# A recurrence and its experts: transposes under sums, four sums moved, narrower turns

## The chip, the cores and the metric

The kernel runs on one core of a Trainium2 chip. The metric is the device time of one execution in microseconds (us), here the median of three runs. Engines are named as in the profile: PE (matmuls), PEld (its weight loads), DVE (vector), ACT (scalar), POOL (GpSimd), SP (issues DMAs).

## The reference

A gated linear recurrence with complex decay feeds a mixture of experts that takes the best one of eight for each token.

```
# B=4 batches, H=8 heads, S=768 steps, D=48
for t in range(S):
    new_re = ar*S_re - ai*S_im ; new_im = ar*S_im + ai*S_re
    S_re, S_im = new_re + k[t] (x) v[t], new_im
    y[t] = q[t] @ S_re
x = y as rows: 3072 tokens of 384
logits = x @ w_gate ; expert = argmax ; gate = softmax of it
for every expert e: rows of its tokens, in order, at most `capacity`
    y_e = relu(rows @ w1[e]) @ w2[e]      # 384 -> 1024 -> 384
out[token] = gate * y_e[its row]
```

## The kernel before

**Units.** The sequence is cut into 8 chunks of 96 steps, so there are 32 units, one for each batch and chunk; batches 0 and 1 come first, alternating, then 2 and 3. A unit loads its decayed q and k (`qkc`, from the scratch `scr`), transposes them per head (`tr`, L348), makes a masked 96x96 product (`pa`, L356), carries the state from chunk to chunk (L369 and after), and sums the output into `py` (L412, L417), with the 384 features in 4 blocks of two heads, each head on 64 partitions of which 48 are used. `take` copies that to `xt` (L590), `logits` multiplies by the gate weights (L612), copies the result to `lt` (L613), and `turn` (L600 to 604) transposes the four blocks back to 96 rows of tokens, which ACT copies to `x`, leaving out the unused columns.

**Order.** The list `SLOT_B` writes out, for one step, which stage of which unit comes next. From the second half of the recurrence to the last unit, PE, DVE, ACT and SP issue in the order of the program (`manual_schedule`); for the experts after that only SP does, and a planner orders the other engines.

**Routing.** After certain chunks `Route.route` runs four stages: R0 `logits` (PE `lg` L681, copy on ACT), R1 `choose` (DVE, L686 to L697), R2 `count` (PE `pp`, L702 and L704) and R3 `place` (DVE, L710 to L713, giving the row `slot` of each token). Rows of tokens are then scattered into `disp` by an indirect DMA of POOL (L622).

**The join.** Expert 0's rows are loaded from `disp` to `xr` (L807) before the last four chunks are there (`LATE`: chunks 7 and 8 of batches 2 and 3). `shift(k)` turns `xr` into PSUM by matmuls against the identity (L831; four blocks of 112 rows for each of the three k). For the late chunks DVE makes a 96x448 matrix of zeros and ones from `slot` (`own`, L821), and `spread` splits the rows into a high and a low part (L639 on ACT, L640 on DVE). `early(k)` adds the first two late chunks onto the same PSUM (two parts each, so four matmuls, L825), `end(k)` the last two, and copies the sum to `xh` and `xl` (L841, L842). In the program all three `shift` follow stage R0 of the last routing; R1, the last splits, R2 and R3 follow; then all `early`, all `end`, then the gates, the counts, and `sort`, whose result says which expert's weights are loaded next.

**Experts.** For each expert, PE turns its rows (`mt`, L911, here by `transpose`), makes `ph` (L973) and `my` (L981), and turns the result back (`yt`, L935).

Of the kernel before, what the change touches and what calls it, by code (L numbers as in the profile page):

```python
# [17 lines left out]
B, H, S, D = 4, 8, 768, 48  # L18
C = 96
DP = 64  # L20
NC = S // C
SIZES = (8, 16, 16, 16, 16, 16, 8)
SL = max(SIZES)
# [4 lines left out]
DM = H * D  # L28
# [24 lines left out]
def crossed(a):  # L53

    p, d = a.ap
    return bass.AP(a.tensor, a.offset, [list(p), [-D, 2], [D, 2], list(d)])


class Att:
# [262 lines left out]
    def unit(self, b, c):  # L322
# [81 lines left out]
        def y():  # L404
# [4 lines left out]
            for i in range(0, H, 2):  # L409
                for h in (i, i + 1):  # L410
                    o = h % 2 * DP
                    nc.tensor.matmul(out=py[o:o + DP, i // 2 * C:i // 2 * C + C], lhsT=v[:, h * D:h * D + DP],  # L412
                                     rhs=a_sb[:, h, :], start=True, stop=c == 0)
# [93 lines left out]
TP = 112  # L507
NT = T // TP
KT = DM // 128
# [8 lines left out]
class Route:  # L518
# [74 lines left out]
    def turn(self, b, c, xt):  # L593

        nc = self.nc
        if b == 3:
            self.x[b] = self.x[0]
        elif b not in self.x:
            self.x[b] = self.x_pool.tile([C, NC, XW], F32, tag="x", name=f"x_{b}", bufs=2)
        pt = self.ps.tile([C, 512], F32, tag="tr", name=f"x_{b}_{c}", bufs=2)  # L600
        for k in range(H // 2):
            nc.tensor.transpose(out=pt[:, k * 128:k * 128 + 128], in_=xt[:, k], identity=self.ident)  # L602
        nc.scalar.copy(out=self.x[b][:, c, :DM].rearrange("t (h e) -> t h e", h=H),
                       in_=pt.rearrange("t (h e) -> t h e", h=H)[:, :, :D])

    def logits(self, b, c, xt, pl):
        nc = self.nc
# [169 lines left out]
class Moe:  # L777
# [31 lines left out]
    def turn_ops(self, ps, chunks, parts, room):  # L809

        nc = self.nc
        acc, own = [], {}
        st = self.first = {t: self.p_0.tile([128, KT, T], F32R, name=f"{t}_0") for t in ("xh", "xl")}

        def find(b, c, slot):
            if len(own) < len(chunks) - 1:
                t = self.p_0.tile([C, T], F32R, name=f"own{len(own)}")
            else:
                t = room.rearrange("p h x -> p (h x)")[:C, :T].bitcast(F32R)
            own[b, c] = t  # L820
            nc.vector.tensor_scalar(out=t, in0=self.number, scalar1=slot, scalar2=None, op0=ALU.is_equal)  # L821

        def add(k, i, stop):
            for z, x in enumerate(parts[chunks[i]]):
                nc.tensor.matmul(out=acc[k][:, :T], lhsT=x[:, k * 128:k * 128 + 128], rhs=own[chunks[i]], start=False, stop=stop and z == 1)  # L825

        def shift(k):
            tag, bufs = (("pa", 2), ("pa", 2), ("s", 1))[k]
            acc.append(ps.tile([128, 512], F32, tag=tag, name=f"mt_0_{k}", bufs=bufs))
            for t in range(NT):  # L830
                nc.tensor.matmul(out=acc[k][:, t * TP:t * TP + TP], lhsT=self.xr[:, t, k * 128:k * 128 + 128],  # L831
                                 rhs=self.ident[:TP, :TP], start=t == 0, stop=False)

        def early(k):
            for i in range(len(chunks) - 2):
                add(k, i, False)

        def end(k):
            for i in range(len(chunks) - 2, len(chunks)):
                add(k, i, i == len(chunks) - 1)  # L840
            nc.scalar.copy(out=st['xh'][:, k], in_=acc[k][:, :T])  # L841
            nc.vector.tensor_tensor(out=st['xl'][:, k], in0=acc[k][:, :T], in1=st['xh'][:, k].bitcast(F32), op=ALU.subtract)  # L842

        def gates():
            st['tail'] = self.p_0.tile([TP, NT, XW - DM], F32, name="tail_0")
            nc.sync.dma_start(out=st['tail'], in_=self.disp[:T, DM:].rearrange("(t p) x -> p t x", p=TP))
        return find, shift, early, end, gates

    def open(self, ctx):
# [407 lines left out]
def kernel(ctx, tc, q, k, v, a_re, a_im, w_gate, w1, w2, out):  # L1257
    nc = tc.nc
    const = ctx.enter_context(tc.tile_pool(name="const", bufs=1))
    dram = ctx.enter_context(tc.tile_pool(name="dram", bufs=1, space=DRAM))  # L1260
    ident = const.tile([128, 128], F32, name="ident")
    flag = const.tile([1, 1], I32, name="flag")
    box = {}
    with ExitStack() as c_main, ExitStack() as c_att:
        cp = c_main.enter_context(tc.tile_pool(name="cp", bufs=1))
        x_pool = c_main.enter_context(tc.tile_pool(name="x_pool", bufs=1))
        att = Att(cp, c_att, tc, dram, ident, q, k, v, a_re, a_im)
        disp = dram.tile([E_ * T, XW], F32, name="disp")
        route = att.route = Route(tc, cp, x_pool, att.ps, ident, disp, w_gate, T, CUTS, LATE)
        with ExitStack() as c_moe:  # L1270
            with ExitStack() as c_dve:
                att.open_dve(c_dve)
                hand = {mybir.EngineType.PE, mybir.EngineType.DVE, mybir.EngineType.Activation, mybir.EngineType.SP}
                slots = att.slots()
                ops = att.dve_ops(slots, 6.5, 10.25)
                with tc.manual_schedule(engines={mybir.EngineType.DVE, mybir.EngineType.Activation}):
                    for op in ops[:att.begin]:
                        op()
                with tc.manual_schedule(engines={mybir.EngineType.DVE}):
                    for op in ops[att.begin:81]:  # L1280
                        op()
                    route.constants()
                    clear = route.clear_ops() + att.clear_ops()
                    for i, op in enumerate(ops[81:att.half], 81):
                        op()
                        if i % 8 == 0 and clear:
                            clear.pop(0)()
                    assert not clear
                with tc.manual_schedule(engines=hand):
                    for op in ops[att.half:]:  # L1290
                        op()
            att.third(c_att)
            moe = Moe(c_moe, tc, ident, disp, w1, w2, out)
            with tc.manual_schedule(engines=hand):
                room = [att.bufs["qkc"][i] for i in range(3)]
                route.room = room[:2]
                route.hook, shift, early, end, gates = moe.turn_ops(att.ps, LATE, route.parts, room[2])
                todo = [(14.5, lambda: nc.vector.memset(room[2][C:], 0.0)), (20, moe.numbers)]
                for p in range(Moe.NP):
                    at = 16 + 3 * p  # L1300
                    todo += [(at, lambda p=p: part(p))]
                todo.sort(key=lambda x: x[0])

                def part(p):
                    loads, splits = moe.weight_ops(0, p)
                    loads[0]()
                    n = 16 + 3 * p
                    todo.extend([(n + 1.5, loads[1]), (n + 2.5, splits[0]), (n + 3, splits[1]), (n + 4, splits[2]), (n + 4.5, splits[3])])
                    todo.sort(key=lambda x: x[0])
                loaded = False  # L1310
                for i, (n, op, _) in enumerate(slots):
                    while todo and todo[0][0] <= n:
                        todo.pop(0)[1]()
                    op()
                    if n > 30.8 and not loaded:
                        moe.load()
                        loaded = True
                    if i == len(slots) - 9:
                        for kk in range(KT):
                            shift(kk)  # L1320
                assert not todo and not route.ready
                for kk in range(KT):
                    early(kk)
                for kk in range(KT):
                    end(kk)
                route.rest()
                while route.ready:
                    route.pace()
                route.totals()
                gates()  # L1330
            route.sort()
            moe.order = route.order
            covered = uncovered(nc, cp, att.sums, att.small, route, flag)
            c_att.close()
            moe.open(c_moe)
            moe.run(lambda: covered(moe.ps))
    go = nc.values_load(flag, min_val=0, max_val=1)
    with tc.If(go > 0):
        General(tc, dram, ident, q, k, v, a_re, a_im, w_gate, w1, w2, out)
# [27 lines left out]
```

## Time and profile before

| | |
|---|---|
| median of three runs | 675.2 us (674.87 to 676.08) |
| the profiled execution's own time | 677.57 us |
| its span, first to last instruction | 675.9 us |
| PE busy | 547.2 us (81%) |
| DVE busy | 481.0 us (71%) |
| ACT busy | 345.8 us (51%) |
| POOL busy | 93.0 us (14%) |
| mean granted clock of PE | 0.923 |

The span is what the trace shows; the 1.67 us between it and the execution's own time lie outside the instructions. A granted clock of 1.00 is 2.4 GHz. Busy shares are means over stages with different limits: the recurrence fills DVE, the later units and the experts fill PE. In the chain views a row's time is what it adds to the chain, from the end of the row before to its own end; in the source and timeline views it is the instruction's own duration, and matmuls overlap.

### The profile page before, as it was taken

How to read it: one execution, taken by the hardware profiler on the slowest of the kernel's cores; microseconds unless marked ns; L12 is line 12 of the kernel's file. 1: busy time of each engine (PE TensorE's matmuls, PEld its weight loads, DVE VectorE, ACT ScalarE, POOL GpSimd, SP SyncE). 2: the span in 40 equal slices, each digit the busy share in tenths (PEclk: the TensorE clock that was granted, in tenths of full speed). 3: DMA queues.
4: the chain of work that ended last, by engine and by line, in shares of the span. 5: the costliest groups of instructions: out<-in, count | busy, mean ns of one | idle time of the engine just before them, and what ended most of it. 6: DMA issues, size and time to landing. Idle time of an engine off the chain costs nothing.

```text
span 675.9 us, 12575 instructions
## 1 busy us (share of the span) xinstructions
PE 547.2 (81%) x4455; PEld 472.2 (70%) x4455; DVE 481.0 (71%) x1432; ACT 345.8 (51%) x789; POOL 93.0 (14%) x140
## 2 busy tenths in 40 slices
PE   0344423366799998989999999999999999999994
PEld 0122211134577877779999988888999999999993
DVE  5999999999999998946757686365555655465431
ACT  6455443475788897644555553254344443443420
POOL 8030000000000000001222222101111202021111
PEclk9876566775999999999999999999999999999998
DMA  5199443585676788687888742483535353626101
GB/s 187 52 312 331 170 140 127 189 236 157 159 240 188 172 225 227 194 206 165 205 231 218 196 122 78 108 258 92 191 107 166 112 165 104 197 74 213 37 35 35
DMA packets 73239, 111.89 MB, mean 166 GB/s; under 512 B 6402, under 2 KB 63045, under 8 KB 71888
## 3 DMA queue, kind: packets, MB, share of 16 engines
q1 hardware_dynamic: 66384, 77.13, 42.0%
q0 software_dynamic: 6784, 33.88, 14.9%
q8 instruction: 37, 0.61, 0.4%
q14 instruction: 34, 0.28, 0.1%
HBM read 72.99 MB, written 34.26 MB: 159 GB/s over the span
## 4 chain that ended last, share of the span: by engine, by line
PE 62%; DVE 17%; ACT 10%; DMA 5%; issue 4%; POOL 1%; SPq 0%; POOLq 0%; DVEq 0%; ACTq 0%
PE ph L973 15%; PE my L981 14%; PE xp L132 5%; PE tr L348 4%; PE pa L356 4%; DVE xy L215 3%; PE s L369 3%; DMA qkc<-scr 3%; PE y L412 3%; DVE a L226 2%; PE y L417 2%; PE x L602 2%; DVE qko L286 2%; PE my L995 2%; PE wp L132 2%
## 5 line engine op out<-in xcount | busy, mean ns | idle before, releaser
L132 PE MATMUL xp<-a,ident 128*128 128x384 f32 x84 | 52.1, 791 | 93.3 <-ACT a L159 93.2
L872 DVE TENSOR_TENSOR lo<-raw,hi 128x384 fp32r<-128x384 f32 (+2 forms) x128 | 66.5, 554 | 64.9 <-ACT hi L871 55.2
L132 PEld LDWEIGHTS xp<-a,ident 128*128 128x128 f32 x84 | 24.4, 307 | 114.6 <-ACT a L159 81.5
L871 ACT CAST hi<-raw 128x384 fp32r<-128x384 f32 (+2 forms) x128 | 60.0, 512 | 55.4 <-PE ph L973 42.5
L215 DVE TENSOR_TENSOR xy<-a 128x96 f32<-128x96 f32 (+1 forms) x301 | 74.9, 279 | 0.7
L348 PE MATMUL tr<-ident,qkc 96*96 96x96 f32 x512 | 65.4, 251 | 9.6 <-DMA qkc<-scr 4.6
L973 PE MATMUL ph<-xh,hi 128*128 128x448 f32 (+4 forms) x192 | 69.7, 365 | 1.1 <-DVE hl L1019 1.1
L973 PE MATMUL ph<-xl,hi 128*128 128x448 f32 (+4 forms) x192 | 67.8, 353 | 0.0
L973 PE MATMUL ph<-xh,lo 128*128 128x448 f32 (+4 forms) x192 | 67.7, 353 | 0.0
L1019 DVE SCALAR_TENSOR_TENSOR hl<-ph,hh 128x448 fp32r<-128x448 f32 (+4 forms) x64 | 37.5, 587 | 39.1 <-ACT hh L1018 38.0
L1018 ACT ACTIVATE hh<-ph 128x448 fp32r<-128x448 f32 (+4 forms) x64 | 32.9, 515 | 61.0 <-PE ph L973 60.6
L981 PE MATMUL my<-hl,hi 128*128 128x448 f32 (+4 forms) x168 | 60.2, 358 | 0.0
L981 PE MATMUL my<-hh,lo 128*128 128x448 f32 (+4 forms) x168 | 59.9, 356 | 0.0
L348 PEld LDWEIGHTS tr<-ident,qkc 96*96 96x96 f32 x512 | 47.5, 128 | 16.6 <-ACT kT L350 7.7
L981 PE MATMUL my<-hh,hi 128*128 128x448 f32 (+4 forms) x168 | 56.2, 361 | 0.1
L226 DVE TENSOR_TENSOR a<-xy 128x48 f32<-128x48 f32 (+1 forms) x298 | 55.3, 215 | 0.4
L356 PE MATMUL pa<-qT,kT 128*96 128x96 f32 x512 | 54.3, 249 | 0.4 <-DVE a_sb L360 0.4
L356 PEld LDWEIGHTS pa<-qT,kT 128*96 128x96 f32 x512 | 49.8, 166 | 1.7 <-issue 1.4
L946 POOL DMA_INDIRECT out_dram<-o,xr x26 | 28.9, 1113 | 157.6 <-DVE o L945 155.8
L622 POOL DMA_INDIRECT disp<-x,idx x32 | 30.2, 943 | 111.6 <-DVE idx L621 59.8
L412 PE MATMUL y<-a_sb,v 128*64 128x96 f32 x512 | 42.3, 253 | 3.9 <-ACT lt L613 2.8
L369 PE MATMUL s<-v,qkc 128*96 128x96 f32 x448 | 44.2, 253 | 0.0
(196 smaller groups left out, 1185.4 us busy)
## 6 DMA issues: line engine op xcount, KB each, us to landing
raw<-in_moe_w_dram SPq DMA_DIRECT2D x64, 384.0 KB
qkc<-scr SPq DMA_DIRECT2D x32, 528.0 KB
scr<-qko POOLq DMA_DIRECT2D x10, 1536.0 KB, 6.8
disp<-fill POOLq DMA_DIRECT2D x7, 772.0 KB, 15.2
v<-in_v_dram SPq DMA_DIRECT2D x32, 144.0 KB
xr<-disp SPq DMA_DIRECT2D x6, 675.5 KB
sx<-s SPq DMA_DIRECT2D x56, 72.0 KB
a<-in_a_re_dram SPq DMA_DIRECT2D x10, 384.0 KB
```

The lines of the kernel that those rows point to most:

```text
L132: nc.tensor.matmul(out=pt[:, :m], lhsT=self.ident, rhs=t[:, h:h + m], start=i == 0, stop=i == 1)
L215: nc.vector.tensor_tensor(out=st['xy'][:, :, cs].rearrange("p (u z) d -> p u z d", u=2), in0=crossed(a4[:, s, 1, cs]), in1=w, op=ALU.mult)
L226: nc.vector.tensor_tensor(out=o, in0=xy[:, 0:4:2, cs], in1=xy[:, 1:4:2, cs], op=ALU.add)
L348: nc.tensor.transpose(out=pt[:, h * C:h * C + C], in_=qk(slice(0, C), 4 * hh + h, slice(z_ * C, z_ * C + C)), identity=self.ident[:C, :C])
L356: nc.tensor.matmul(out=pa[:, h * C:h * C + C], lhsT=kT[:, 4 * hh + h], rhs=qT[:, 4 * hh + h], start=True, stop=True)
L369: nc.tensor.matmul(out=ps[:, h * D:h * D + C], lhsT=qk(slice(None), h, slice(C, 2 * C)), rhs=v[:, h * D:h * D + C], start=True, stop=True)
L412: nc.tensor.matmul(out=py[o:o + DP, i // 2 * C:i // 2 * C + C], lhsT=v[:, h * D:h * D + DP], rhs=a_sb[:, h, :], start=True, stop=c == 0)
L871: nc.scalar.copy(out=hi[i][:, s], in_=raw[i][:, s])
L872: nc.vector.tensor_tensor(out=lo[i][:, s], in0=raw[i][:, s], in1=hi[i][:, s].bitcast(F32), op=ALU.subtract)
L973: nc.tensor.matmul(out=ph[:, :WIDTHS[e]], lhsT=a[:, k, fs], rhs=r[:, k, :WIDTHS[e]], start=k == 0 and i == 0, stop=k == KT - 1 and i == 2)
L981: nc.tensor.matmul(out=py[m][:, :WIDTHS[e]], lhsT=a[:, f % self.PF, ms], rhs=r[:, :WIDTHS[e]], start=f == 0 and i == 0, stop=f == NF - 1 a ...
L1019: nc.vector.scalar_tensor_tensor(out=hl[:, :w], in0=ph[:, :w], scalar=0.0, in1=hh[:, :w].bitcast(F32), op0=ALU.max, op1=ALU.subtract)
```

## The change

`turn` transposes 112 partitions instead of 128 (the second head of a block ends at 64 + 48 = 112), so each transpose writes 112 columns; the helper `paired` gives ACT the pattern of the used columns. The matmuls of `shift` are marked as transposes; the sums of `early` and `end` go on top of them as before. `early(0)`, the four sums of the first k, is issued right after `shift`, ahead of R1 to R3 of the last routing.

```diff
+PW = DP + D
...
+def paired(a):
+
+    p, d = a.ap
+    return bass.AP(a.tensor, a.offset, [list(p), [PW, H // 2], [DP, 2], list(d)])
...
         for k in range(H // 2):
-            nc.tensor.transpose(out=pt[:, k * 128:k * 128 + 128], in_=xt[:, k], identity=self.ident)
-        nc.scalar.copy(out=self.x[b][:, c, :DM].rearrange("t (h e) -> t h e", h=H),
-                       in_=pt.rearrange("t (h e) -> t h e", h=H)[:, :, :D])
+            nc.tensor.transpose(out=pt[:, k * PW:k * PW + PW], in_=xt[:PW, k], identity=self.ident[:PW, :PW])
+        nc.scalar.copy(out=self.x[b][:, c, :DM].rearrange("t (k u e) -> t k u e", u=2, e=D), in_=paired(pt[:, :D]))
...
                 nc.tensor.matmul(out=acc[k][:, t * TP:t * TP + TP], lhsT=self.xr[:, t, k * 128:k * 128 + 128],
-                                 rhs=self.ident[:TP, :TP], start=t == 0, stop=False)
+                                 rhs=self.ident[:TP, :TP], start=t == 0, stop=False, is_transpose=True)
...
                         for kk in range(KT):
                             shift(kk)
+                        early(0)
                 assert not todo and not route.ready
-                for kk in range(KT):
+                for kk in range(1, KT):
                     early(kk)
```

## Rows read from the trace of the kernel before

**Rows 1.** Page, part 4: shares of the chain that ended last.
```profile
PE 62%; DVE 17%; ACT 10%; DMA 5%; issue 4%; POOL 1%; SPq 0%; POOLq 0%; DVEq 0%; ACTq 0%
```

**Rows 2.** Windows: length; busy us (instructions) PE, PEld, DVE, ACT, POOL; PEclk, DMA, GB/s.
```profile
22.00:120.00 98.00, 36.89 (x72) 18.53 (x73) 95.40 (x359) 46.78 (x81) 8.38 (x14) 0.67 0.60 199
220.00:240.00 20.00, 19.26 (x230) 16.64 (x229) 19.57 (x49) 16.97 (x52) 0.53 (x1) 1.00 0.75 191
330.00:350.00 20.00, 20.00 (x292) 18.39 (x290) 10.91 (x28) 10.63 (x26) 5.59 (x6) 1.00 0.89 224
417.00:425.00 8.00, 8.00 (x55) 7.59 (x55) 4.61 (x19) 2.18 (x8) 1.26 (x2) 1.00 0.14 40
441.00:460.00 19.00, 18.83 (x99) 16.85 (x99) 10.53 (x23) 9.13 (x21) 0.00 (x0) 1.00 0.78 232
500.00:600.00 100.00, 100.00 (x555) 95.97 (x554) 54.92 (x108) 43.51 (x95) 18.33 (x15) 1.00 0.47 142
```

**Rows 3.** Waits of PE, 300 to 416: us in total, times, longest.
```profile
PE x L602 <- ACT qT L350: 0.8, 3, 0.3
```

**Rows 4.** The chain in order of time, 260 to 335: start, us, what.
```profile
292.38 6.10 DMA qkc<-scr
...
306.07 0.57 PE x L602 x4
```

**Rows 5.** Source view, L602, 298 to 417: duration ns min/median/max, first and last start.
```profile
L602 PE MATMUL x<-ident,xt x76: 272/273/315, 299.4 to 416.3; 128*96 128x128 f32 x76
```

**Rows 6.** The chain, 425 to 520.
```profile
425.52 0.62 DVE xl L842
...
441.33 2.09 PE ph L973 x9
...
448.92 0.39 PE mt L911 x4
...
474.04 0.33 PE yt L935 x3
```

**Rows 7.** ACT by shape, 298 to 417: busy us, mean ns, idle before.
```profile
L350 ACT COPY kT<-tr 96x384 f32<-96x384 f32 x32 | 15.2, 475 | 14.0 <-PE tr L348 13.8
...
L603 ACT COPY x<-x 96x384 f32<-96x384 f32 x19 | 9.0, 476 | 6.2 <-PE x L602 6.1
```

**Rows 8.** The chain, 330 to 480, at the join.
```profile
415.97 0.57 PE x L602 x4
...
416.89 2.77 PE mt L831 x24
419.75 0.17 PE pp L704 x2
419.93 5.00 PE mt L825 x24
```

**Rows 9.** Timeline of ACT, 411 to 432: start, us.
```profile
416.26 0.23 ACT L613 COPY lt<-y 128x96 f32<-128x96 f32 x1
```

**Rows 10.** Source view of L911, whole run.
```profile
L911 PEld LDWEIGHTS mt<-ident,xr x78: 135/140/144, 444.5 to 634.9; 112*128 112x128 f32 x48, 128*128 128x128 f32 x18, 80*128 80x128 f32 x6, 96*128 96x128 f32 x3
```

**Rows 11.** Timeline of DVE, 411 to 432.
```profile
415.98 1.02 DVE L640 TENSOR_TENSOR qkc<-x,qkc 96x384 fp32r<-96x384 f32 x2 [0.38 <-ACT qkc L639]
...
418.26 0.16 DVE L696 TENSOR_TENSOR sl<-sl,oh 96x8 f32<-96x8 f32 x1
...
418.54 1.02 DVE L640 TENSOR_TENSOR qkc<-x,qkc 96x384 fp32r<-96x384 f32 x2
419.96 0.17 DVE L710 TENSOR_TENSOR sl<-pp,lim 96x16 f32<-96x16 f32 x1 [0.41 <-PE pp L704]
...
420.78 0.45 DVE L821 TENSOR_SCALAR own<-number,slot 96x448 fp32r<-96x448 f32 x1
421.14 0.44 DVE L821 TENSOR_SCALAR qkc<-number,slot 96x448 fp32r<-96x448 f32 x1
```

**Rows 12.** Source view of L132, 20 to 120.
```profile
L132 PE MATMUL wp<-qko,ident x40: 486/486/1009, 22.7 to 120.0; 128*128 128x384 f32 x40
```

## The prediction

> **What bounds it now.** I read the chain that ended last first: PE has 62% of it, DVE 17% [rows 1]. Since a share of the whole says nothing about one stage, I then took windows [rows 2]. At 220 to 240 DVE is busy 19.57 of 20 us: a shorter PE instruction buys little there. At 330 to 350 PE is busy 20.00 of 20, from 417 to 425 8.00 of 8, and in the experts 18.83 of 19 and 100.00 of 100. From 300 to 416 no wait of PE is on a DMA; the largest is 0.8 us, on ACT copies that themselves follow PE [rows 3]. The chain has its last DMA wait before the join at 292.38 + 6.10 = 298.5; the units after it run on PE [rows 4]. So time taken off PE after 298.5 should come off the end. At the join the chain is PE without a gap: turn of the last rows, 24 records of `shift`, the count, 24 sums [rows 8]; then ACT, DVE, routing, scatter, weights, and PE again at 441.33 [rows 6], each step released by the one before. There the reader is to see that what the join gains moves this whole tail.
>
> **112 columns.** No row shows this transpose at 112, but others give the cost of one more in a run: in `yt`, which writes 128 columns, three take 0.33 us, 0.110 each; in `mt`, which writes 112, four take 0.39, 0.0975 each [rows 6]. So four save 4 x 0.0125 = 0.05 us a unit; the bounds are 0, if the weight load sets the pitch, and 128 - 112 of 128 columns of the group's 0.57 us [rows 4], 0.07. I take 0.05, as the two rows are the same operation. After 298 there are 76 records, one a transpose, thus 19 units [rows 5]. The last one is hidden: the gate sums behind it wait for `lt`, which ACT ends at 416.26 + 0.23 = 416.49, while the turn itself ends at 415.97 + 0.57 = 416.54 with its last starts earlier [rows 8, 9]. 18 x 0.05 = 0.90 us; bounds 0 and 1.3. The 13 units before 298 lie beside a full DVE, which is their cover; without it they would be worth 13 x 0.05 = 0.65. I take 0.1, bounds 0 and 0.65.
>
> ACT reads PSUM in one more stride. Its copy with gaps takes 476 ns now, a contiguous one of the same size 475 [rows 7], so gaps cost nothing and I take the new pattern at nothing. A slower copy would have cover too: ACT waits for this turn 6.1 us in 19 copies, 0.32 us each [rows 7]. Without that cover each 0.1 us would cost up to 1.9.
>
> **Transposes in `shift`.** Twelve matmuls make 24 records, 2.77 us [rows 8]. The same shape as a transpose stands in the experts: 48 records of 112x128 [rows 10], one a call, four in 0.39 us. Twelve: 12 x 0.0975 = 1.17 us, 1.60 less. Bounds: if a run of twelve goes at its weight loads one behind another, 12 x 0.140 [rows 10] = 1.68 and 1.09 less; nothing less, if the flag changes nothing (a rival below). I take 1.17, for four in a row run at that pitch inside other matmuls.
>
> **What is late next.** `shift` begins at 416.89 and now ends at 418.06. The next in PE's queue is `early(0)`, four sums at 5.00 / 24 = 0.208 us [rows 8], 0.83 in all. This is a new wait on the first pair of splits, which DVE ends at 415.98 + 1.02 = 417.00 [rows 11], 1.06 us before it is needed. Were they later than that, the count, queued behind, and the whole of R3 would be late by as much. `early(0)` ends at 418.89. The count needs `sl`, done at 418.26 + 0.16 = 418.42 [rows 11], so it follows at once; it took 419.93 - 419.66 = 0.27 and ends at 419.16. Without the four sums PE would have idled from 418.06 to 418.42 or so: this idle time covers half of the move.
>
> Now DVE is late: R3 stands behind the second pair of splits, until 418.54 + 1.02 = 419.56. Before, R3 began at 419.96 after 0.41 us of waiting for the count; now it can begin at 419.57, 0.39 earlier. Its end, the first `own`, comes 420.78 + 0.45 - 419.96 = 1.27 us later [rows 11], at 420.84, and the second at 421.14 + 0.44 - 0.39 = 421.19.
>
> PE runs the eight other early sums from 419.16 to 420.83. `end(0)` needs the first `own` at 420.84; with the step from DVE to PE I put 0.1 us of waiting there. Its third sum, at 421.35, finds the second `own` ready. Twelve sums end at 420.93 + 2.50 = 423.43, before at 419.93 + 5.00 = 424.93: 1.50 us gained. With no wait for `own` it is 1.60; with the slow run of twelve, 1.09 (PE then never waits for `own`). SP and POOL issue nothing in the moved pieces; the scatters keep their order and come earlier with DVE.
>
> **The sum.** 0.90 + 0.10 + 1.50 = 2.50 us, on the profiled execution's 677.57 (span 675.9): 675.07. The median of the runs, 675.2, lies 2.4 below that execution; I take the same 2.5 off it: 672.7. About 0.2%, 1.35 us, is what a measurement tells from no change; the forecast is 0.37%.
>
> **A rule against it.** At 330 to 350 the granted clock is 1.00, 2.4 GHz, although a unit, which takes (416.3 - 299.4) / 18 = 6.5 us, has 16 transposes in `tr` and 4 in `turn` by the code: some 60 of the 292 records of those 20 us [rows 2, 5]; at 22 to 120, with PE busy 37 of 98 us, it is 0.67 [rows 2], and the same matmul goes from 486 to 1009 ns [rows 12]. The Trainium skill, page "TensorE: Matmul & The Clock Gate", section "Part 4: PE-mode transpose", says that transposes do not count as work for the clock in the way matmuls do. By that rule, `shift` as transposes could let the clock fall; the stretch of many transposes at 1.00 speaks against it here, and its price is a rival.
>
> **Rivals.**
> 1. Only the join pays: the columns are hidden, because the period of a unit is held elsewhere, most likely by the transfers, whose share of DMA time is 0.89 at 330 to 350 [rows 2]. Against it: no wait on them [rows 3]. 675.2 - 1.5 = 673.7.
> 2. The experts lose it again: there the order is a planner's, and earlier starts may set turns and splits elsewhere. The chain there has little slack, 0.17 us idle in 441 to 460 and none in 500 to 600 [rows 2], so a new order can hardly gain, and a unit of loss is a missed product of one k, a turn of 0.39 [rows 6] or an `xl` of 0.62 [rows 6]. Two of the latter: 675.2 - 2.5 + 1.2 = 673.9; three, 674.5. I take 674.2.
> 3. The flag does not do what it says, since sums come on top: `shift` keeps 24 records and 2.77 us. Then `early(0)` ahead of the count puts R3 off by 0.83; the first `own` comes at 422.06, the early sums end at 419.93 + 0.83 + 1.67 = 422.43, so the move costs nothing and gains nothing. 675.2 - 1.0 = 674.2.
> 4. Slower: the clock falls to 1.2 GHz behind `shift`, and the 24 sums go at 1009 / 486 = 2.08 of their time: 5.00 x 1.08 = 5.4 us more. It decides from the point where over 2.5 / 1.08 = 2.3 us of PE's work are done at the low clock. 675.2 - 2.5 + 5.4 = 678.1. For it: the last transposes of the units stand directly ahead. Against it: 417 to 425 has no gap [rows 2].
>
> **How the numbers follow.** The forecast has a chance of 0.68. The bounds of its three terms together make 675.2 - (1.3 + 0.65 + 1.6) = 671.65 and 675.2 - (0 + 0 + 1.09) = 674.1; as they need not all fall on one side, its own range is 671.9 to 673.5. Rival 1 has 0.10, rival 2 0.11, rival 3 0.05, rival 4 0.06. Range 671.8 to 674.3: it holds the forecast, rivals 1 and 3 and most of 2. Faster means under 673.85: nearly all of the forecast, most of rival 1, a quarter of rival 2, together 0.76; slower is rival 4 and a worse case of 2, 0.07; the same, 0.17.
>
> **What would show it.** In the profile after: `shift` with 12 records in about 1.2 us of the chain; the turns of the units with 112 columns and 0.52 a group, ACT's copy still near 476 ns; four sums ahead of the count; DVE going from the last split to R3 without the 0.41 us of waiting; PE waiting under 0.2 us for `own`; last sum to 441.33's counterpart unchanged at 16.4 us; experts as long as before, at clock 1.00. Wrong it would be if `shift` kept 24 records, if PE stood for the first splits ahead of `early(0)`, if a unit's period stayed the same, or if the experts took longer.

## The result, and the profile after

The changed kernel takes 680.05 us (median of 8 runs, 678.09 to 684.53), the kernel before, on the same chip, 675.35 us (8 runs, 674.5 to 677.47). The ratio is 1.0066, 95% interval 1.0044 to 1.0087: slower, where 0.37% faster was forecast and the range ended at 674.3. The profiled execution took 680.47 us, with a span of 678.8 us (before 675.9) and a mean granted clock of 0.917 (before 0.923).

The chain of the changed kernel at the join, to be held against [rows 8] (start, us, what):

```profile
414.09 0.52 PE x L609 x4
414.61 0.40 PE lg L687 x4
415.01 1.20 PE mt L837 x12
416.21 0.82 PE mt L831 x4
417.31 4.35 PE mt L831 x20
421.68 0.54 ACT xh L847
422.25 0.62 DVE xl L848
```

The last turn, now at line 609, adds 0.52 us instead of 0.57. `shift` (now L837) has 12 records in 1.20 us instead of 24 in 2.77. `early(0)` follows it without a gap, four sums in 0.82. The last sum ends at 417.31 + 4.35 = 421.66; before it ended at 419.93 + 5.00 = 424.93. So the changed kernel leaves the join 3.27 us ahead, more than the 2.50 forecast for it, and it ends 2.9 us behind. Between the two, 6.2 us are lost. (Of the 3.27, 0.9 is an earlier start of the late units, which moves by more than that between profiles of unchanged units; see **Columns** below. The 6.2 stand behind the join and do not depend on it.) The same chain goes on:

```profile
425.91 2.59 DMA disp<-x,idx
428.52 0.33 SPq L852
428.89 0.49 SPq L887
429.68 5.11 DMA xr<-disp
434.84 1.20 PE mt L917 x5
436.03 3.39 PE ph L979 x9
439.42 1.89 PE my L987 x8
441.31 1.82 PE ph L979 x9
```

A transfer of 5.11 us stands in the chain, the load of expert 1's rows, and PE is idle until it ends. The kernel before has a transfer in its chain at this place too, of expert 1's weights:

```profile
433.49 5.55 DMA raw<-in_moe_w_dram
```

There PE works on expert 0 meanwhile and waits only 0.17 us at the end of that chain, at 441.33. In the changed kernel, behind the load, come five of expert 1's row transposes in 1.20 us (four took 0.39), and a `ph` of nine matmuls in 3.39 us, where the next but one takes 1.82. In the rows that follow, `hh` and `hl` are the high and the low part of relu(`ph`), which ACT and DVE make and `my` reads; `hi` and `lo` are the same split of the weights `raw`. The waits of PE in the changed kernel, 417 to 446 (us in total, times, longest), and its timeline there:

```profile
PE mt L917 <- DMA xr<-disp: 4.4, 1, 4.4
PE ph L979 <- DVE hl L1025: 0.4, 1, 0.4
```

```profile
429.68 0.78 PE L987 MATMUL my<-hh,hi 128*128 128x448 f32 x3
434.84 1.20 PE L917 MATMUL mt<-ident,xr 112*128 112x112 f32 x5 [4.37 <-DMA xr<-disp]
435.71 0.72 PE L979 MATMUL ph<-xh,hi 128*128 128x448 f32 x1
436.23 0.57 PE L979 MATMUL ph<-xl,hi 128*128 128x448 f32 x1
```

Windows of the changed kernel (columns as in [rows 2]):

```profile
417.00:425.00 8.00, 8.00 (x44) 7.13 (x43) 5.90 (x31) 2.14 (x4) 0.31 (x1) 1.00 0.07 21
430.00:435.00 5.00, 0.63 (x4) 0.25 (x3) 0.00 (x0) 0.00 (x0) 0.00 (x0) 0.80 0.84 223
435.00:441.00 6.00, 6.00 (x22) 5.46 (x23) 3.35 (x7) 3.43 (x8) 0.00 (x0) 0.60 1.08 361
441.00:460.00 19.00, 19.00 (x99) 17.15 (x98) 9.47 (x21) 7.72 (x17) 0.00 (x0) 1.00 0.47 135
```

The kernel before, in two of these stretches:

```profile
430.00:435.00 5.00, 5.00 (x26) 4.60 (x26) 1.25 (x2) 0.55 (x1) 0.10 (x1) 1.00 0.33 57
435.00:441.00 6.00, 5.96 (x29) 4.97 (x27) 1.28 (x3) 1.37 (x3) 0.00 (x0) 1.00 1.08 331
```

Here the reader sees both halves of the price. From 430 to 435 PE of the changed kernel has 0.63 us of work; the granted clock falls to 0.80 in this stretch and is 0.60 in the next, although PE is busy all of it. At 441 it is back at 1.00.

Why PE stands there is in the view of the tile `xr`, 425 to 447. First the changed kernel, then the kernel before (duration ns min/median/max, first and last start):

```profile
L917 PE MATMUL mt<-ident,xr x9: 257/394/450, 434.8 to 445.3; 112*128 112x112 f32 x9
L908 SPq DMA_DIRECT2D xr<-disp x2: 340/342/345, 429.7 to 443.3; - x2
```

```profile
L911 PE MATMUL mt<-ident,xr x4: 258/258/260, 444.7 to 445.0; 112*128 112x112 f32 x4
L902 SPq DMA_DIRECT2D xr<-disp x2: 340/342/344, 432.9 to 444.8; - x2
```

In the kernel before, SP issues the load of expert 1's rows at 432.9 and PE asks for them at 444.7, 11.8 us later. In the changed kernel the load is issued earlier, at 429.7, but PE asks for the rows at once and gets them at 434.8. Nothing in the diff touches this line. What moved is its place in PE's queue. The instruction streams of the two compiled kernels, from the count on (the name, and how many matmuls):

```
before  pcount ph*18 my*3 ph*9 my*9 ph*9 my*8 ph*9 my*9 ph*9 my*7 mt*4 ph*9 ...
after   pcount ph*18 my*3 ph*9 my*9 mt*5 ph*9 ...
```

Before, expert 1's first turn (`mt`) stands behind six groups of nine `ph` of expert 0, after behind three. ACT's stream moved as well: before, the first three `hh` of expert 0 precede the split (`hi`, L871) of expert 1's weights; after, only two do, and the third `hh` stands behind a split that waits for its own transfer. In these stages the planner orders PE, ACT and DVE and only SP keeps to the program.

### The profile page after: what moved, and what is told of

Read it like the earlier page. It is cut to its first block, busy times and chain, and to the rows that moved or that the text cites. A ratio compares the mean times of both kernels' runs of the same rounds, so it can differ in the third digit from the quotient of the medians.

```text
span 678.8 us, 12552 instructions
## 1 busy us (share of the span) xinstructions
PE 543.8 (80%) x4443; PEld 470.0 (69%) x4443; DVE 480.8 (71%) x1432; ACT 345.9 (51%) x789; POOL 92.7 (14%) x140
## 4 chain that ended last, share of the span: by engine, by line
PE 62%; DVE 18%; ACT 9%; DMA 5%; issue 4%; POOL 1%; SPq 0%; POOLq 0%; DVEq 0%; ACTq 0%
PE ph L979 16%; PE my L987 14%; PE xp L139 5%; PE pa L363 4%; PE tr L355 4%; DVE xy L222 4%; PE s L376 3%; PE y L419 3%; DVE a L233 3%; DVE qko L293 2%; PE y L424 2%; PE my L1001 2%; PE x L609 2%; DMA qkc<-scr 2%; DVE a L203 2%
## 5 line engine op out<-in xcount | busy, mean ns | idle before, releaser
L139 PE MATMUL xp<-a,ident 128*128 128x384 f32 x84 | 50.0, 762 | 93.9 <-ACT a L166 93.8
```

The source lines that it names most:

```text
L139: nc.tensor.matmul(out=pt[:, :m], lhsT=self.ident, rhs=t[:, h:h + m], start=i == 0, stop=i == 1)
```

## The experiments

The order theory (theory A of the last four expectations): the join's gain is real, and the whole loss is the planner's new order in the experts. The main rival: one of the edited parts is itself dear. Others are named where they are expected. Each run below has its own ratio, to the kernel before on the same chip, over 4 to 12 runs against 23 or 33 of before, with a 95% interval; medians of before differ from set to set (675.35 to 678.09), so only ratios are compared.

| run | what it has | ratio | interval |
|---|---|---|---|
| flag_alone | flag | 0.998 | 0.9967 to 0.9993 |
| cols_alone | 112 columns | 1.0104 | 1.0088 to 1.012 |
| early_alone | moved sums | 1.0092 | 1.0076 to 1.0107 |
| flag_early | flag, moved sums | 0.9981 | 0.9967 to 0.9995 |
| after_pin | the change, PE's turns held | 1.0036 | 1.0021 to 1.005 |
| cols_pin | 112 columns, PE's turns held | 1.0063 | 1.0049 to 1.0077 |
| early_pin | moved sums, PE's turns held | 1.0048 | 1.0034 to 1.0062 |
| before_pin | the kernel before, PE's turns held | 1.0001 | 0.9988 to 1.0013 |
| after_hold | the change, PE, ACT and DVE held | 0.9961 | 0.9945 to 0.9976 |
| cols_hold | 112 columns, all three held | 0.9985 | 0.9968 to 1.0002 |
| early_hold | moved sums, all three held | 0.9994 | 0.998 to 1.0008 |
| flagcols_hold | flag and 112 columns, all three held | 0.9979 | 0.9962 to 0.9995 |

### The change with PE's turns held, and the parts alone

The hold ties expert 1's turns on PE to their place in the program, and changes no other line:

```diff
-                nc.tensor.transpose(out=pt[:, t * TP_:t * TP_ + r], in_=st['xr'][:r, t, k * 128:k * 128 + 128],
-                                    identity=self.ident[:r, :r])
+                ins = nc.tensor.transpose(out=pt[:, t * TP_:t * TP_ + r], in_=st['xr'][:r, t, k * 128:k * 128 + 128],
+                                          identity=self.ident[:r, :r])
+                if e == 1:
+                    self.tc.keep_in_program_order(ins)
```

> The changed kernel, but expert 1's twelve row transposes are held behind the PE instructions that stand before them in the program, so they come some two steps of expert 0 later, as in the kernel before. Theory (order): the loss is PE standing 4.37 us for expert 1's rows, because the planner put these transposes too early, and then 4 us at the low clock. Then PE has no wait on the rows, the clock stays 1.00 from 417 to 460, and the time is 675.35 - 3.3 (the join's last sum ends at 421.66 instead of 424.93) = 672.1. Rival (work): the transposes under sums, or the narrower turns, cost in themselves: 678 or more. Rival (clock): transposes let the clock fall: it falls here too, 676 or more.

Measured: 680.2 us against 677.85, ratio 1.0036. This is less than the change loses (1.0066, with intervals that overlap a little), but not the gain that the order theory wanted. PE's wait for the rows is gone, and another has come. Waits of PE, 428 to 446, and the timeline of ACT in after_pin:

```profile
PE my L989 <- ACT hh L1026: 3.0, 1, 3.0
```

```profile
434.42 0.62 ACT L877 CAST hi<-raw 128x512 fp32r<-128x512 f32 x1 [9.33 <-DMA raw<-in_moe_w_dram]
434.95 0.54 ACT L1026 ACTIVATE hh<-ph 128x448 fp32r<-128x448 f32 x1
```

ACT stands 9.33 us for the weights of expert 1, and the `hh` of expert 0 that PE needs for `my` is queued behind it. Behind that wait too the granted clock is low, 0.72 from 435 to 441. So the order theory in its first form, the order on PE alone, fell: ACT's order was moved as well, and PE's wait for the rows had hidden that.

The flag and the moved sums, without the columns:

```diff
+                                 rhs=self.ident[:TP, :TP], start=t == 0, stop=False, is_transpose=True)
...
+                        early(0)
                 assert not todo and not route.ready
-                for kk in range(KT):
+                for kk in range(1, KT):
                     early(kk)
```

> The kernel before with the transposes in shift and the moved early(0), but turns of 128 columns. Its plan puts expert 1's row transposes where the kernel before has them. Theory (order): no wait on the rows, the join gains 1.5: 673.8. Rival (work): if the transposes under sums cost, 679 or more, as the changed kernel. If only the narrow turns cost, also 673.8.

Measured: 676.86 against 677.85, 0.9981 (0.9967 to 0.9995). Its streams have the order of the kernel before, and it is faster.

The moved sums alone (the diff above without the flag's line), and the columns alone (two of the lines):

```diff
-            nc.tensor.transpose(out=pt[:, k * 128:k * 128 + 128], in_=xt[:, k], identity=self.ident)
+            nc.tensor.transpose(out=pt[:, k * PW:k * PW + PW], in_=xt[:PW, k], identity=self.ident[:PW, :PW])
...
+        nc.scalar.copy(out=self.x[b][:, c, :DM].rearrange("t (k u e) -> t k u e", u=2, e=D), in_=paired(pt[:, :D]))
```

> The kernel before with early(0) moved ahead of the count and nothing else. The move itself should cost nothing, but its plan puts expert 1's row transposes early, as in the changed kernel. Theory (order): PE waits about 4.4 us for the rows and then runs at the low clock, with no gain at the join to set against it: 681 to 682. Rival (work) with the cost in the transposes or in the narrow turns: 675.4, as before.

> The kernel before with turns of 112 columns and nothing else. Its plan also puts expert 1's row transposes early. Theory (order): 675.35 - 1.0 + 6 = 680 to 681, the wait on the rows again about 4.4 us. Rival (work) with the cost in the transposes of shift: 674.4; with the cost in the narrow turns: slower, but with no wait on the rows.

Measured: 683.79 and 684.32 against 677.85, 1.0092 and 1.0104. The columns alone are dearer than the whole change, the moved sums alone at least as dear (the intervals overlap). The order theory had 681 to 682 and 680 to 681 on a kernel before of 675.35, ratios of 1.0084 to 1.0098 and 1.0069 to 1.0084: it holds for the moved sums, and the columns lost more than it said, with a longer wait. The waits of PE, first in early_alone, then in cols_alone:

```profile
PE mt L911 <- DMA xr<-disp: 3.9, 1, 3.9
```

```profile
PE mt L917 <- DMA xr<-disp: 5.0, 1, 5.0
```

Both have the early turn in their streams, and both wait for the same transfer; in cols_alone the granted clock from 435 to 441 is 0.58. Four sums in another place and sixteen columns fewer share no instruction; what they share is the new order behind them.

### Parts with PE's turns held, the flag alone, and the hold alone

The edits are the diffs above: the columns and the hold, the moved sums and the hold, the flag's line alone, and the hold alone on the kernel before.

> Turns of 112 columns alone, with expert 1's row transposes held back as in after_pin. Theory (order): the columns' own worth shows, 675.35 - 1.0 = 674.4. Rival (the columns are hidden): 675.35. Rival (work, the narrow turns cost): above 676.

> early(0) moved and nothing else, with expert 1's row transposes held back. Theory (order): the loss of early_alone goes away in full, 675.35 give or take 0.5. Rival (the moved sums make the count late): 676 or more.

> Only shift's matmuls marked as transposes; its plan leaves expert 1's row transposes late. The join without the moved sums: shift 1.6 shorter, PE then idles up to 0.4 us ahead of the count: 1.1 to 1.3 us gained, 674.1. Against flag_early it gives the worth of the moved sums, 0.2 to 0.4.

> The kernel before with the same hold on expert 1's row transposes, which its plan already has late. A control: 675.35, no change. If it is faster or slower, the hold itself does something and the other pinned runs have to be read against this one.

Measured: cols_pin 682.2, early_pin 681.04, flag_alone 676.25 and before_pin 678.07, all against 677.72. The hold costs nothing by itself (1.0001). With it, cols_pin and early_pin lose less than without, but the order theory, with PE's order alone, had expected 674.4 and 675.35 on a kernel before of 675.35; both missed, as after_pin did. PE waits for ACT's `hh` instead of the rows, 3.4 and 2.1 us:

```profile
PE my L989 <- ACT hh L1026: 3.4, 1, 3.4
```

```profile
PE my L983 <- ACT hh L1020: 2.1, 1, 2.1
```

The flag alone keeps the order of the kernel before and gives 0.998. Its chain at the join:

```profile
414.93 0.57 PE x L602 x4
415.50 0.35 PE lg L681 x4
415.85 1.20 PE mt L831 x12
417.05 0.11 issue
417.15 0.34 PE pp L702 x2
417.50 0.28 PE pp L704 x2
417.77 5.01 PE mt L825 x24
```

From the last turn's start to the last sum's end it takes 422.78 - 414.93 = 7.85 us, before 424.93 - 415.97 = 8.96 [rows 8]: 1.11 us. In flag_early the same stretch takes 7.63 us, so the moved sums add 0.22 there, too little for the runs to show (0.9981 against 0.998).

### All three engines held

Now the splits of expert 1's first two parts are also tied, on ACT and DVE, behind the third and fourth `hh` and `hl` of expert 0, their place in the kernel before:

```diff
+            if e == 1 and p < 2:
+                for x, y in zip(ins, self.made[2 + p]):
+                    self.tc.add_manual_dep(x.ins, y.ins.name, mybir.DependencyInfo(
+                        mybir.DependencyClass.NoSync, mybir.DependencyReason.DATA), reason="behind a step of the first expert")
```

Here `ins` are the two instructions of a split and `made` keeps the `hh` and `hl` instructions of the steps. No wait is added or taken away; only places in queues are set. The streams of the experts then are those of the kernel before. This second hold was not run on the kernel before by itself; the nearest to that is early_hold below.

The other three have the columns, the moved sums, or the flag and the columns, with this hold.

> The changed kernel whole, with two things held: the row turns of expert 1 stay in program order on PE, and the weight splits of expert 1's first two parts stay on ACT and DVE behind the third and fourth hidden step of expert 0, where the kernel before has them. Theory A (the whole loss is the order in the experts on PE, ACT and DVE; the join's gain of 3.3 us is real): 3.3 us under before, ratio 0.995 (0.993 to 0.997), no wait of PE on xr or hh over 0.5 us from 428 to 445, granted clock 1.00 from 430 on. Rival B (something else in the experts is late, such as the weights of expert 1, so the earlier start is given back whatever the order): ratio 0.999 to 1.001, with PE waiting later for hi of expert 1. Rival C (the order isn't the cause): 1.004 to 1.007 as without the hold.

> The 112 columns alone, with the same hold on expert 1's turns and splits. Without a hold these columns alone cost 1.0104, with the turns alone held 1.0063. Theory A: the 18 units give 0.05 us each, so 0.9 us, ratio 0.9985 (0.997 to 1.000). Rival B (the earlier start is given back later): 1.000. Rival C: 1.006 as with the turns alone held.

> Four sums ahead of the count alone, with the same hold. Without a hold 1.0092, with the turns alone held 1.0048. Theory A: by the run with the flag and the moved sums, which was no faster than the flag alone, the move is worth about nothing by itself: 1.000 (0.998 to 1.002). Rival C (the moved sums themselves make the routing late): 1.003 or more, and the count later in the profile than in before.

> Flag and 112 columns without the moved sums, with the same hold. The flag alone gave 0.998 (1.3 us). Theory A: flag 1.3 us and columns 0.9 us add: ratio 0.9967 (0.995 to 0.998); what after_hold has beyond this is the moved sums' worth, forecast by the join at up to 1 us. If flagcols_hold equals after_hold, the moved sums are worth nothing on top of the flag.

Measured, against 678.09: after_hold 675.32, cols_hold 677.55, early_hold 677.9, flagcols_hold 676.95. Each ratio lies in the range of theory A, though the interval of cols_hold does not part it from its rival B (1.000). The whole change with the order held is 0.9961 (0.9945 to 0.9976), and its rivals B (0.999 to 1.001) and C (1.004 or more) are out. In after_hold PE's windows have no hole and no low clock, its chain has the join's gain, and expert 1's rows are asked for late again, at 440.7, 11.6 us after their load was issued at 429.1:

```profile
430.00:435.00 5.00, 5.00 (x26) 4.63 (x25) 0.00 (x0) 0.00 (x0) 0.00 (x0) 1.00 1.00 281
435.00:441.00 6.00, 5.83 (x30) 4.79 (x30) 4.65 (x10) 5.07 (x12) 0.00 (x0) 1.00 1.04 343
```

```profile
413.54 0.52 PE x L609 x4
...
414.45 1.20 PE mt L837 x12
415.66 0.83 PE mt L831 x4
416.76 4.34 PE mt L831 x20
...
437.35 2.08 PE ph L985 x9
```

```profile
L921 PE MATMUL mt<-ident,xr x8: 257/258/260, 440.7 to 445.1; 112*128 112x112 f32 x8
```

From the end of the last sum, 416.76 + 4.34 = 421.10, to the `ph` at 437.35, the first behind the weights' transfer, it takes 16.25 us, before 16.40 (424.93 to 441.33 [rows 6]). Its profiled span is 671.9 us.

The rival that an edited part is itself dear is out with cols_hold and early_hold: neither is slower than before, and flag_alone was faster without any hold. What the single parts are worth is less sharp. The interval of cols_hold reaches 1.0002, and early_hold is no change; those of flagcols_hold and flag_alone overlap, and so do those of flagcols_hold and after_hold.

## Why the prediction was wrong

**The step that failed** is the term of the experts. The sum put it at nothing ("experts as long as before"), and rival 2, the only place where it had a price, priced it far too low. That rival had the right mechanism, a planner that sets turns and splits elsewhere, but I took as its unit of loss a missed product, a turn or an `xl`, 0.39 to 0.62 us, two or three of them, and gave it a chance of 0.11. The runs showed another unit: the landing of a transfer for which PE waits, and the slow work behind it. The changed kernel's own rows give four terms; what each takes without the loss is from [rows 6], from the next `ph` and from sums at 1.00. PE is idle for 4.37 us. The five turns at the low clock take 1.20 instead of 5 x 0.0975 = 0.49, the nine `ph` 3.39 instead of 1.82, eight `my` 1.89 instead of 8 x 0.205 = 1.64. That is 4.37 + 0.71 + 1.57 + 0.25 = 6.90. The 6.2 that are lost are less, since PE waits less for `hl`: 0.5 us in the whole of 430 to 640, before 1.1. By runs, the order alone is worth 1.0066 / 0.9961 = 1.0105, some 7 us (1.0068 to 1.0143 from the ends of both intervals); the same quotient is 1.0119 for the columns alone and 1.0098 for the moved sums alone.

The prediction read "0.17 us idle in 441 to 460" as little slack, so that a new order could hardly gain, and then priced a loss by single instructions [rows 2]. That is slack of the engine. The slack that mattered is between a transfer and its first reader: 11.8 us in the kernel before, of which the load, by the changed kernel's chain, needs about 5.1. It was in the trace, in the source view of L902 and L911, and nothing but the planner's order kept it.

**Why the order changed** is only argued, not shown. That the planner puts the turn ahead of three steps which need no transfer, and ACT's split likewise, fits a planner which takes the loads as landed earlier than the chip lands them. Which edits tip it follows no plain rule here: the flag does not, nor does the flag with the moved sums; the columns do, the moved sums do, and so does the whole change.

**Columns.** In the trace pair sized right; the runs alone do not show it. The group takes 0.52 as forecast, and ACT's copy into `x` 475 ns, so the stride cost nothing. The 19 last turns span 298.5 to 414.4, 115.9 us, before 116.9 [rows 5]: 1.0 against 0.90. This stretch scatters by more than that from profile to profile (116.9 to 119.3 in seven without the columns, 115.9 to 119.3 in seven with them; medians 119.0 and 117.7), so the trace pair alone would not carry it. The medians and cols_hold, 0.9985 +- 0.0017, agree with it, but the interval of cols_hold holds 1.000 as well. The stretch also starts 0.9 us earlier; profiles of unchanged units start it anywhere from 295.5 to 299.4, so I count that for nothing, and no run shows the 0.10 for the earlier units.

**Transposes in `shift`.** Right: 12 records, 1.20 us against 1.17, and the four sums right behind take 0.82 / 4 = 0.205 each, before 0.208. Rival 3 is out. Rival 4 too: 417 to 425 is at 1.00 with PE full.

**What is late next.** Mostly right. The timeline of DVE in the changed kernel:

```profile
416.63 1.02 DVE L646 TENSOR_TENSOR qkc<-x,qkc 96x384 fp32r<-96x384 f32 x2
417.57 0.16 DVE L716 TENSOR_TENSOR sl<-pp,lim 96x16 f32<-96x16 f32 x1
...
418.37 0.45 DVE L827 TENSOR_SCALAR own<-number,slot 96x448 fp32r<-96x448 f32 x1
```

DVE goes from the last split to R3 without the 0.41 us of waiting [rows 11], and the first `own` is there at 418.82. The 20 sums take 4.35 instead of 20 x 0.208 = 4.17: the wait for `own`, put at 0.1, is 0.18 at most. From turn to last sum 421.66 - 414.09 = 7.57 us against 8.96: 1.39, forecast 1.50. For the moved sums on top of the flag, the prediction's own numbers give 0.26 (0.36 of idle time saved, 0.1 of waiting for `own`); flag_early and flag_alone give 0.22 in the trace. Without the flag they are worth nothing that the runs can tell (early_hold).

**The tail** is where "each step released by the one before" was taken as the whole of it. Up to `sort` and the scatter that held; then steps of expert 0 that were not late at all were queued behind a step of expert 1 that waited for its transfer.

**The sum** of 2.50 us, 0.9963, is what after_hold measures with the order held: 0.9961 (0.9945 to 0.9976). Rival 1, the join alone (673.7, that is 0.9978), lies just outside that interval.

## What to carry to other kernels

Where a planner sets the order, a change upstream is also a change of the order downstream, and small shifts tip it: compare the instruction streams of both kernels stage by stage before the price of the edit is believed. For each transfer that has a late first reader, read the time from its issue to that reader; if only the order keeps that distance, price its loss at the transfer's landing plus the work that then runs at a low clock, and hold the order if the edit is to be judged by itself. A held order must cover every queue: with PE held alone, ACT's queue made the next wait.

## What the runs showed of the hardware

After PE had stood for 4.37 us, 435 to 441 went at a mean granted clock of 0.60, of which 434.8 to 439.4 at 0.50, that is 1.2 GHz: there matmuls of `ph` started 0.38 us apart (436.23, 436.61), where nine in 1.82 us make 0.20 at 1.00, 2.4 GHz. This added 2.5 us to the wait of 4.4. In cols_alone the clock was 0.50 from 437.6, where a wait of 5.0 ended, to 441, in early_alone 0.50 from 439.5, after one of 3.9, to 443. The Trainium skill, "TensorE: Matmul & The Clock Gate", "HAM oscillation — how this bites in real kernels", says that a wait for a transfer between groups of matmuls lets the clock fall, so that the work behind it starts slow; the traces agree, with these numbers.

Transposes as the first writers of a PSUM group, with fp32 sums added onto them, went at 0.10 us each, against 0.23 for the same block as a matmul (1.20 / 12 and 2.77 / 12).
